# A reordered prologue: block 1's norm and half of the first B norm on VectorE, block 0's attention output stored in four parts

## The chip, the cores and the metric

The kernel runs on one core of a Trainium2 chip. The metric is the device time of one execution in microseconds (us). Executions of this kernel agree within about 0.2%. A comparison calls a version faster or slower only if it differs by more than 2%.

## The reference, cut to what matters

Two pairs of layers on 2048 tokens of width 1024: A is a dilated local attention with 32 heads and a window of 8 keys (every second token), B is a gated MLP of width 3584. Both stand behind a layer norm without parameters and add to the residual x.

```python
def _layernorm(x, axis=-1, eps=1e-5):
    m = jnp.mean(x, axis=axis, keepdims=True)
    v = jnp.var(x, axis=axis, keepdims=True)
    return (x - m) / jnp.sqrt(v + eps)
...
    x = A_x
    x = x + _A_ref(_layernorm(x, axis=-1), A_wqkv, A_wo)
    x = x + _B_ref(_layernorm(x, axis=-1), B_W_gate, B_W_up, B_W_down)
    x = x + _A_ref(...)      # the same again
    x = x + _B_ref(...)
```

## The kernel before

Tokens are worked on in four blocks of 512; a block has four tiles of 128 tokens (`TPB = 4`). The kernel is one list of timed events, `ev`: each step is a function with the time at which its author expects it, and the instructions are emitted in order of these times. TensorE's matmul groups and all transfers issued by SyncE are chained (`issue_after`), so each of these two queues runs strictly in the order of the list. A transfer that waits for its data holds back every transfer listed behind it.

The norm of a block, as it runs on ScalarE, with GpSimd computing (variance + eps) to the power −0.5; `turn` is the transposing transfer that makes the matmul operand `xnT` from the normalised `xn`:

```python
    def ln_steps(n, which, early=False):
        ...
        def stats(t):
            def f():
                ...
                nc.scalar.activation(xn, xt[:], ACT.Square, accum_out=sq)
                nc.scalar.activation(xn, xt[:], ACT.Identity, accum_out=sx)
                ...
                nc.gpsimd.tensor_tensor(rstd, vpe, neg_half[:, 0:1], op=ALU.pow)
                nc.scalar.activation(mr, sx, ACT.Copy, scale=-1.0 / D)
                nc.scalar.activation(nb, mr, ACT.Identity, scale=rstd)
            return f

        def apply(t):
            def f():
                nc.scalar.activation(hold["xn"][:, t, :], x_tiles[b * TPB + t][:], ACT.Identity,
                                     scale=hold["st"][:, t, 4:5], bias=hold["st"][:, t, 6:7])
            return f

        def turn(t=None):
            def f():
                if t is not None:
                    sp_dma(hold["xnT"][:, t, :, :], hold["xn"][:, t, :], True)
                else:
                    ...
```

The attention output of a block goes to DRAM and comes back transposed (`oT`), to be the operand of the output projection:

```python
    def store_o(n):
        def f():
            b = n % NB
            dst = bass.AP(tensor=o_d.tensor, offset=o_d[b * TPB:b * TPB + 1].offset, ap=[[DH * P, P], [1, DH * P]])
            sp_dma(dst, att[n]["o_hm"][:].rearrange("p d t -> p (d t)"))
        return f
```

The prologue of the schedule. `want_...` asks for 1 MB slabs of weights; its times say when the ring slot of a slab comes free, and with that where the load of a later slab stands in SyncE's queue. `ln1` is the norm ahead of an attention block, `ln2` the one ahead of the MLP ("B norm"), `sums1` are the products of q and k of block 1, on VectorE:

```python
    spread(v_steps(0, ln_a[0], "v0", early=True), t_v0, GRP)
    ln1(1, 22.0, 47.5, True, 5.0)
    ...
    ev.append((t_qk1 + 1.6 * GRP, lambda: softmax(0)))
    spread(pv_steps(0), t_qk1 + 10.0, 4.2)
    ln1(2, 60.0, t_qk1 + 15.0, True)
    ...
    want_v("v123", t_v3 + GRP * KC / 2, t_gu0)
    spread(v_steps(1, ln_a[1], "v123", True), t_v1, GRP)
    ln1(3, 85.0, t_v2 + 2.0, True)
    ...
    spread(v_steps(2, ln_a[2], "v123", True), t_v2, GRP)
    ev.append((t_v2 + 10.0, store_o(0)))
    ev.append((t_v2 + 10.1, load_o(0)))
    ...
    spread(sums1, t_qk1 + 46.0, 4.4)
    want_wo(0, t_v3, t_v3)
    spread(wo_steps(0), t_wo0, 2 * GRP)
    ln2(0, [t_wo0 + 2 * GRP * (t + 1) + 0.1 for t in range(TPB)])
    spread(v_steps(3, ln_a[3], "v123"), t_v3, GRP)
    ...                       # then the gate and up groups of the MLP of block 0
```

So TensorE's order in the stretch that matters is: V of blocks 1 and 2, output projection of block 0, V of block 3, first gate group, first up group, and from there on the long MLP.

## Time and profile before

The time before is 1652.67 us (median of 3 runs, 1652.44 to 1653.47). The profiled execution spans 1650.2 us. Two lines of its page: TensorE's busy time, and the shares of the chain of waits that ended last.

```profile
PE 1623.2 (98%) x7576; PEld 778.2 (47%) x7576; DVE 1048.1 (64%) x888; ACT 534.6 (32%) x1117; POOL 276.3 (17%) x220
...
PE 90%; issue 0%; DVE 0%; ACT 0%; DMA 0%
```

TensorE is busy 98% of the span, and 90% of the chain is TensorE. So there is little to gain but TensorE's waits and its slow stretches. These are TensorE's waits other than the start-up ones and two short ones, 0.7 and 0.5 us, ahead of logit reductions (the tile that the matmul makes, what it waited for, us in total, times, longest):

```profile
PE acc_wo L115 <- DMA oT<-o_d: 6.5, 1, 6.5
PE acc_g L115 <- issue: 2.4, 1, 2.4
PE acc_v L115 <- ACT vT L303: 1.7, 1, 1.7
```

And this is TensorE's timeline around them. The columns are start, duration, engine, line, what is made from what, how many matmuls of which form, and in brackets the wait before it:

```profile
92.88 13.98 PE L115 MATMUL acc_v<-xnT_a,w_v 128*128 128x512 bf16 x64
108.50 13.97 PE L115 MATMUL acc_v<-xnT_a,w_v 128*128 128x512 bf16 x64 [1.65 <-ACT vT L303]
129.03 16.73 PE L115 MATMUL acc_wo<-w_o,oT 128*128 128x512 bf16 x64 [6.55 <-DMA oT<-o_d]
145.59 13.98 PE L115 MATMUL acc_v<-xnT_a,w_v 128*128 128x512 bf16 x64
161.96 3.53 PE L115 MATMUL acc_g<-xnT_b,w_g 128*128 128x512 bf16 x8 [2.40 <-issue]
165.33 1.89 PE L115 MATMUL acc_u<-xnT_b,w_u 128*128 128x512 bf16 x8
```

Read the 64 matmuls of the output projection (`acc_wo`) against the 64 of V (`acc_v`): 16.73 us against 13.98, though they have the same form. They follow a wait of 6.55 us. The first 8 gate matmuls (`acc_g`) follow a wait of 2.40 us and take 3.53 us, the next group 1.89. A wait can cost twice: itself, and a slow clock after it. In windows of 1 us the granted clock was one half from the first matmul to about 165.3 us at the gate group (3.4 us), but to about 134.6 us at the projection (5.6 us). **From the first up group (165.33 us) to the end of the span are 1484.9 us**; this number will serve as a check on every version.

The first gate group waits for the last transposed tile of the B norm. In ScalarE's timeline the last `xn_b` is ready at 158.71 us; its transpose, issued at 158.74, took 3.1 us to land, and the group starts at 161.96. SyncE's queue shows that tile's transpose right behind it, alone, while the third gate slab had been issued 13 us before it:

```profile
145.78 0.37 SPq L104 DMA_DIRECT2D w_g<-in_B_W_gate_dram  x1
...
158.74 1.23 SPq L104 DMA_TRANSPOSE xnT_b<-xn_b  x1
```

### The profile page before, as it was taken

The numbers are of one execution on the slowest core, as the hardware profiler recorded it, in microseconds if no ns is written. First come the engines' busy times: TensorE is split into PE (matmuls) and PEld (weight loads), VectorE is DVE, ScalarE is ACT, GpSimd is POOL, SyncE is SP. The second block draws the span as 40 slices with busy tenths as digits, with TensorE's granted clock in tenths as the row PEclk, the third lists the DMA queues.
The fourth block names the chain that finished last, engine by engine and source line by source line (L and its number), as shares of the span: only waits on it lengthen the run. The fifth ranks groups of instructions, "written<-read, shape, count | busy, mean of one in ns | idle before, by whom it ended". The sixth has DMA issues, their size and how long they took to land.

```text
span 1650.2 us, 18654 instructions
## 1 busy us (share of the span) xinstructions
PE 1623.2 (98%) x7576; PEld 778.2 (47%) x7576; DVE 1048.1 (64%) x888; ACT 534.6 (32%) x1117; POOL 276.3 (17%) x220
## 2 busy tenths in 40 slices
PE   7998999999999999999999999999999999999999
PEld 4543445444454445444454444544445444444444
DVE  1798788978199844949459493694927948211211
ACT  6675412415132522325124151340513401131110
POOL 1341104401052101211042010420105100000000
PEclk9998999999999999999999999999999999999999
DMA  7477666764747474784846847477485774655451
GB/s 257 104 192 193 163 172 190 206 190 148 231 149 190 152 204 142 229 210 136 211 155 202 200 153 223 160 187 199 153 229 178 186 219 152 198 160 184 153 163 67
DMA packets 370791, 296.82 MB, mean 180 GB/s; under 512 B 142352, under 2 KB 351248, under 8 KB 369680
## 3 DMA queue, kind: packets, MB, share of 16 engines
q1 hardware_dynamic: 370416, 295.10, 62.3%
q8 instruction: 59, 0.97, 0.2%
q10 hardware_dynamic: 288, 0.52, 0.1%
q14 instruction: 28, 0.23, 0.0%
HBM read 256.77 MB, written 21.00 MB: 168 GB/s over the span
## 4 chain that ended last, share of the span: by engine, by line
PE 90%; issue 0%; DVE 0%; ACT 0%; DMA 0%
PE acc_g L115 24%; PE dacc L115 23%; PE acc_u L115 23%; PE acc_wo L115 6%; PE acc_k L115 5%; PE acc_q L115 5%; PE acc_v L115 3%; PE L L115 0%; DVE x L556 0%; ACT vT L303 0%; DMA xnT_b<-xn_b 0%
## 5 line engine op out<-in xcount | busy, mean ns | idle before, releaser
L115 PE MATMUL acc_g<-xnT_b,w_g 128*128 128x512 bf16 x1792 | 425.0, 380 | 2.4 <-issue 2.4
L115 PE MATMUL acc_u<-xnT_b,w_u 128*128 128x512 bf16 x1792 | 423.3, 379 | 0.0
L115 PE MATMUL dacc<-w_d,hT 128*128 128x512 bf16 x1792 | 388.1, 379 | 0.0
L528 ACT ACTIVATE r<-acc_g 128x512 bf16<-128x512 f32 x224 | 132.6, 594 | 699.4 <-PE acc_g L115 685.1
L529 DVE TENSOR_TENSOR hT<-acc_u,r 128x512 bf16<-128x512 f32 x224 | 153.5, 687 | 322.0 <-PE acc_u L115 308.3
L115 PEld LDWEIGHTS <-w_g 128*128 128x128 bf16 x1792 | 175.0, 98 | 216.4 <-issue 7.5
L115 PEld LDWEIGHTS <-w_u 128*128 128x128 bf16 x1792 | 175.4, 98 | 211.8 <-issue 0.6
L115 PEld LDWEIGHTS <-hT 128*128 128x128 bf16 x1792 | 175.3, 98 | 211.4
L399 DVE TENSOR_TENSOR t<-q,k 128x2048 f32<-128x2048 bf16 x98 | 223.6, 2289 | 9.8 <-ACT k L342 6.6
L409 DVE TENSOR_TENSOR ac<-ac,t 128x2048 f32<-128x2048 f32 x84 | 191.8, 2283 | 0.4
L347 POOL COPY kh<-k 128x14 bf16<-128x14 bf16 x64 | 85.5, 1341 | 452.4 <-ACT k L342 452.4
L556 DVE TENSOR_TENSOR x<-dacc,x 128x512 bf16<-128x512 f32 x64 | 42.5, 687 | 164.8 <-PE dacc L115 164.8
L461 DVE TENSOR_TENSOR pv<-a,vhm 128x4096 bf16<-128x4096 bf16 x64 | 145.2, 2282 | 0.0
L115 PE MATMUL acc_wo<-w_o,oT 128*128 128x512 bf16 x512 | 114.6, 385 | 6.5 <-DMA oT<-o_d 6.5
L223 POOL TENSOR_TENSOR st_b<-st_b,neg_half 128x1 f32<-128x1 f32 x32 | 66.4, 2080 | 323.0 <-ACT st_b L222 323.0
L223 POOL TENSOR_TENSOR st_a<-st_a,neg_half 128x1 f32<-128x1 f32 x36 | 51.4, 1427 | 359.1 <-ACT st_a L222 359.1
L115 PEld LDWEIGHTS <-oT 128*128 128x128 bf16 x512 | 50.6, 99 | 69.3 <-DMA oT<-o_d 7.3
L346 POOL COPY k<-kh 128x14 bf16<-128x14 bf16 x48 | 71.8, 1497 | 45.6 <-DVE t L399 45.6
L462 DVE TENSOR_TENSOR pv<-pv 128x2048 bf16<-128x2048 bf16 x64 | 77.4, 1215 | 0.2
L218 ACT ACTIVATE xn_b<-x 128x1024 bf16<-128x1024 bf16 x32 | 33.4, 1045 | 96.5 <-DVE x L504 96.5
L338 ACT CAST q<-acc_q 128x512 bf16<-128x512 f32 x64 | 37.4, 584 | 71.2 <-PE acc_q L115 71.2
L399 DVE TENSOR_TENSOR ac<-q,k 128x2048 f32<-128x2048 bf16 x14 | 32.0, 2287 | 39.9 <-ACT k L342 32.8
(121 smaller groups left out, 1190.8 us busy)
## 6 DMA issues: line engine op xcount, KB each, us to landing
w_g<-in_B_W_gate_dram SPq DMA_DIRECT2D x56, 1024.0 KB, 6.8
w_u<-in_B_W_up_dram SPq DMA_DIRECT2D x56, 1024.0 KB, 5.4
w_d<-in_B_W_down_dram SPq DMA_DIRECT2D x48, 1024.0 KB, 5.6
w_o<-in_A_wo_dram SPq DMA_DIRECT2D x16, 1024.0 KB, 7.3
vhm<-v_d SPq DMA_DIRECT2D x32, 284.0 KB, 6.8
v_d<-vT SPq DMA_DIRECT2D x8, 1024.0 KB, 8.5
o_d<-ohm SPq DMA_DIRECT2D x8, 1024.0 KB, 10.0
oT<-o_d SPq DMA_DIRECT2D x32, 256.0 KB, 4.2
```

Source lines behind the costliest of these rows:

```text
L115: tail_pe[0] = nc.tensor.matmul(*args, **kwargs).ins
L223: nc.gpsimd.tensor_tensor(rstd, vpe, neg_half[:, 0:1], op=ALU.pow)
L338: nc.scalar.copy(q[:], acc[:])
L346: nc.gpsimd.tensor_copy(k[:, 0:HALO], khalo[n - 1][:, c, :])
L347: nc.gpsimd.tensor_copy(khalo[n][:, c, :], k[:, BLK:BLK + HALO])
L399: nc.vector.tensor_tensor(t[:], i0, i1, op=ALU.mult)
L409: nc.vector.tensor_tensor(o, ac[:], t[:], op=ALU.add)
L461: nc.vector.tensor_tensor(tt[:], a_bc, v_sh, op=ALU.mult)
L462: nc.vector.tensor_tensor(tt[:, 0:4], tt[:, 0:4], tt[:, 4:8], op=ALU.add)
L528: nc.scalar.activation(r[:], acc[:], ACT.Relu)
L529: nc.vector.tensor_tensor(hold["hT"][:, j, :], accs["u"][:], r[:], op=ALU.mult)
L556: nc.vector.tensor_tensor(xs, ac[t], xs, op=ALU.add)
```

## The change

The intent: block 1's norm moves from ScalarE to VectorE, which idled from 13.5 to 39.4 us; the norms of blocks 2 and 3 move forward into the time so gained on ScalarE; tiles 2 and 3 of the first B norm go to VectorE and most of block 1's products move behind them; the attention output is stored in four parts, so that only the last quarter follows the last P·V step; transposes of the B norm are listed 2.5 us earlier. The core of the diff:

```diff
@@ ln_steps: stats(t) and apply(t)
+                if t in dve:
+                    hold[t] = ln_dve_stats(xt)
+                    return
...
+                if t in dve:
+                    mv, rstd = hold[t]
+                    nc.vector.tensor_scalar(hold["xn"][:, t, :], x_tiles[b * TPB + t][:], mv[:, 0:1], rstd[:],
+                                            op0=ALU.subtract, op1=ALU.mult)
+                    return
...
+    def ln_dve_stats(xt):
+        bst = stat_pool.tile([P, 2, 6], F32, tag="bst", name="bst")
+        nc.vector.bn_stats(bst[:, 0, :], xt[:, 0:512])
+        nc.vector.bn_stats(bst[:, 1, :], xt[:, 512:1024])
+        ...
+        nc.gpsimd.tensor_tensor(rstd[:], vpe[:], neg_half[:, 0:1], op=ALU.pow)
+        return mv, rstd
...
-    def store_o(n):
+    def store_o(n, g0=0, g1=NG):
...
-                ev.append((a + 9.0, turn(t)))
+                ev.append((a + 6.5, turn(t)))
...
-    ln1(1, 22.0, 47.5, True, 5.0)
+    ln1(1, 18.0, t_qk0 + 2.0, True, 2.6, range(TPB))
...
-    spread(pv_steps(0), t_qk1 + 10.0, 4.2)
-    ln1(2, 60.0, t_qk1 + 15.0, True)
+    ln1(2, 36.0, t_qk1 + 2.0, True, 5.0)
+    spread(pv_steps(0), t_qk1 + 12.0, 4.2)
+    for i in range(4):
+        ev.append((t_qk1 + 12.0 + 9.0 * (i + 1) + 1.0, store_o(0, 2 * i, 2 * i + 2)))
+    ev.append((t_qk1 + 12.0 + 9.0 * 4 + 1.1, load_o(0)))
+    ln1(3, 66.0, t_v2 + 9.5, True, 5.0)
...
-    ln1(3, 85.0, t_v2 + 2.0, True)
-    ev.append((t_v2 + 10.0, store_o(0)))
-    ev.append((t_v2 + 10.1, load_o(0)))
...
-    spread(sums1, t_qk1 + 46.0, 4.4)
+    spread(sums1[:5], t_qk1 + 50.0, 4.4)
+    spread(sums1[5:], t_v3 + 6.0, 4.4)
...
-    ln2(0, [t_wo0 + 2 * GRP * (t + 1) + 0.1 for t in range(TPB)])
+    ln2(0, [t_wo0 + 2 * GRP * (t + 1) + 0.1 for t in range(TPB)], None, (2, 3))
```

(The loads of x of blocks 2 and 3, the stores of V and the requests for slabs were moved in the list as well.)

More of the change, by code (lines that the diff above doesn't have):

```diff
@@ L202, in slab_events, with ln_steps @@
             events.append((slab_plan[i - RING][2] + 0.3 if i >= RING else 0.1 * i, f))
-    def ln_steps(n, which, early=False):
+    def ln_steps(n, which, early=False, dve=()):
         b = n % NB
@@ L243, in ln_steps @@
         return [stats(t) for t in range(TPB)], [apply(t) for t in range(TPB)], turn, hold
+    def ln_dve_stats(xt):
+        bst = stat_pool.tile([P, 2, 6], F32, tag="bst", name="bst")
+        nc.vector.bn_stats(bst[:, 0, :], xt[:, 0:512])
+        nc.vector.bn_stats(bst[:, 1, :], xt[:, 512:1024])
+        mv = stat_pool.tile([P, 2], F32, tag="mv", name="mv", bufs=4)
+        nc.vector.bn_aggr(mv[:], bst[:].rearrange("p a b -> p (a b)"))
+        vpe = stat_pool.tile([P, 1], F32, tag="vpe1", name="vpe1")
+        nc.vector.tensor_scalar(vpe[:], mv[:, 1:2], EPS, None, op0=ALU.add)
+        rstd = stat_pool.tile([P, 1], F32, tag="rstd1", name="rstd1", bufs=4)
+        nc.gpsimd.tensor_tensor(rstd[:], vpe[:], neg_half[:, 0:1], op=ALU.pow)
+        return mv, rstd
     def ln_first():
@@ L251, in ln_first @@
             if t % 2 == 0:
-                bst = stat_pool.tile([P, 2, 6], F32, tag="bst", name="bst")
-                nc.vector.bn_stats(bst[:, 0, :], xt[:, 0:512])
-                nc.vector.bn_stats(bst[:, 1, :], xt[:, 512:1024])
-                mv = stat_pool.tile([P, 2], F32, tag="mv", name="mv")
-                nc.vector.bn_aggr(mv[:], bst[:].rearrange("p a b -> p (a b)"))
-                vpe = stat_pool.tile([P, 1], F32, tag="vpe1", name="vpe1")
-                nc.vector.tensor_scalar(vpe[:], mv[:, 1:2], EPS, None, op0=ALU.add)
-                rstd = stat_pool.tile([P, 1], F32, tag="rstd1", name="rstd1")
-                nc.gpsimd.tensor_tensor(rstd[:], vpe[:], neg_half[:, 0:1], op=ALU.pow)
+                mv, rstd = ln_dve_stats(xt)
                 nc.vector.tensor_scalar(xn, xt[:], mv[:, 0:1], rstd[:], op0=ALU.subtract, op1=ALU.mult)
@@ L271, in ln_first @@
                 nc.vector.tensor_scalar(vpe[:], nvar[:], -1.0 / D, EPS, op0=ALU.mult, op1=ALU.add)
-                rstd = stat_pool.tile([P, 1], F32, tag="rstd1", name="rstd1")
+                rstd = stat_pool.tile([P, 1], F32, tag="rstd1", name="rstd1", bufs=4)
                 nc.gpsimd.tensor_tensor(rstd[:], vpe[:], neg_half[:, 0:1], op=ALU.pow)
@@ L467, in pv_steps @@
         return [f_(g) for g in range(NG)]
-    def store_o(n):
+    def store_o(n, g0=0, g1=NG):
         def f():
             b = n % NB
-            dst = bass.AP(tensor=o_d.tensor, offset=o_d[b * TPB:b * TPB + 1].offset, ap=[[DH * P, P], [1, DH * P]])
-            sp_dma(dst, att[n]["o_hm"][:].rearrange("p d t -> p (d t)"))
+            off = g0 * DG * P
+            size = (g1 - g0) * DG * P
+            dst = bass.AP(tensor=o_d.tensor, offset=o_d[b * TPB:b * TPB + 1].offset + off, ap=[[DH * P, P], [1, size]])
+            sp_dma(dst, att[n]["o_hm"][:].rearrange("p d t -> p (d t)")[:, off:off + size])
         return f
@@ L587, in zero_v, with ln1 @@
         sp_dma(bass.AP(tensor=v_d.tensor, offset=v_d.offset, ap=[[NTOK, P], [P * NTOK, KC], [1, HALO]]), zpad[:])
-    def ln1(n, at, turn_at, early=False, gap=3.0):
-        stats, apply, turn, hold = ln_steps(n, "a", early)
+    def ln1(n, at, turn_at, early=False, gap=3.0, dve=()):
+        stats, apply, turn, hold = ln_steps(n, "a", early, dve)
         ln_a[n] = hold
@@ L594, in ln1, with ln2 @@
         ev.append((turn_at, turn()))
-    def ln2(n, ats, turn_at=None):
-        stats, apply, turn, hold = ln_steps(n, "b")
+    def ln2(n, ats, turn_at=None, dve=()):
+        stats, apply, turn, hold = ln_steps(n, "b", False, dve)
         ln_b[n] = hold
@@ L608 @@
     GAP0 = 2.05
-    t_v0 = 15.0
+    t_v0 = 17.0
     t_qk0 = t_v0 + GRP * KC
@@ L616 @@
     t_gu0 = t_v3 + GRP * KC
-    ev.append((0.45, zero_v))
-    ev.append((0.5, lambda: load_x(1)))
     want_v("v0", t_v0 + GRP * KC / 2, t_qk0)
     want_qk("qk01", t_v1)
+    want_v("v123", t_v3 + GRP * KC / 2, t_gu0)
+    ev.append((0.45, lambda: load_x(1)))
+    ev.append((0.5, zero_v))
     spread(v_steps(0, ln_a[0], "v0", early=True), t_v0, GRP)
-    ln1(1, 22.0, 47.5, True, 5.0)
+    ln1(1, 18.0, t_qk0 + 2.0, True, 2.6, range(TPB))
+    ev.append((t_qk0 - 4.0, lambda: load_x(2)))
     ev.append((t_qk0 + 1.5, store_v(0)))
+    ev.append((t_qk0 + 2.1, lambda: load_x(3)))
     spread(qk_steps(0, ln_a[0], "qk01"), t_qk0, GAP0)
@@ L631 @@
     spread(load_v_steps(0), t_qk0 + 5.0, 6.0)
-    ev.append((50.0, lambda: load_x(2)))
-    spread(qk_steps(1, ln_a[1], "qk01"), t_qk1, GRP)
     ev.append((t_qk1 + 0.5 * GRP, reds[KC - 2]))
@@ L636 @@
     ev.append((t_qk1 + 1.6 * GRP, lambda: softmax(0)))
-    spread(pv_steps(0), t_qk1 + 10.0, 4.2)
-    ln1(2, 60.0, t_qk1 + 15.0, True)
-    ev.append((70.0, lambda: load_x(3)))
-    want_v("v123", t_v3 + GRP * KC / 2, t_gu0)
+    ln1(2, 36.0, t_qk1 + 2.0, True, 5.0)
+    spread(qk_steps(1, ln_a[1], "qk01"), t_qk1, GRP)
+    spread(pv_steps(0), t_qk1 + 12.0, 4.2)
[3 more added lines that the diff above has]
+    ln1(3, 66.0, t_v2 + 9.5, True, 5.0)
     spread(v_steps(1, ln_a[1], "v123", True), t_v1, GRP)
-    ln1(3, 85.0, t_v2 + 2.0, True)
-    ev.append((t_v2 + 3.0, store_v(1)))
+    ev.append((t_v2 + 9.6, store_v(1)))
     spread(v_steps(2, ln_a[2], "v123", True), t_v2, GRP)
-    ev.append((t_v2 + 10.0, store_o(0)))
-    ev.append((t_v2 + 10.1, load_o(0)))
     ev.append((t_wo0 + 3.0, store_v(2)))
     sums1, red1 = prod_sum_steps(1)
-    spread(sums1, t_qk1 + 46.0, 4.4)
+    spread(sums1[:5], t_qk1 + 50.0, 4.4)
+    spread(sums1[5:], t_v3 + 6.0, 4.4)
     want_wo(0, t_v3, t_v3)
     spread(wo_steps(0), t_wo0, 2 * GRP)
-    ln2(0, [t_wo0 + 2 * GRP * (t + 1) + 0.1 for t in range(TPB)])
+    ln2(0, [t_wo0 + 2 * GRP * (t + 1) + 0.1 for t in range(TPB)], None, (2, 3))
     spread(v_steps(3, ln_a[3], "v123"), t_v3, GRP)
```

## The prediction

> **What bounds the kernel now.** Engine shares: TensorE busy 1623 of 1650 us (98%). The chain of waits is 90% TensorE. Nothing can gain 2% (33 us) without fewer matmuls, and the change removes none: TensorE's order of groups stays identical. Only idle and slow time in the first 165 us is at stake. The waits and the TensorE timeline show it: some 12 us at start-up (untouched), 1.2 us at two logit reductions (40 to 47 us), 1.65 us at the V projection of block 2 (V copies queued on ScalarE behind block 3's norm), 6.55 us ahead of the output projection (oT, read back from DRAM), 2.4 us ahead of the first gate matmul (transpose of xn_b). After the last two, matmuls start 0.43 us apart instead of 0.216: the output projection's 64 took 16.7 us against 14.0, the first gate group 3.5 against 1.9. The Trainium skill, "TensorE: Matmul & The Clock Gate", Part 1, says an idle TensorE falls to half clock and needs about 3.4 us to recover; this trace agrees. At stake: about 16 us (1%).
>
> **What the change does.**
> 1. Block 1's norm goes to VectorE (per tile two statistics at 0.6 us, a 0.54 us apply), idle from 13.5 to 39 us: free. The norms of blocks 2 and 3 (about 4.2 us a tile on ScalarE) move forward to 30 to 77 us; with the copies (0.47 us each) they fill ScalarE there. The 1.65 us wait goes.
> 2. ScalarE's last norm steps wait for GpSimd's power operation, which sits out VectorE's two-input operations ([...]the skill, "SBUF — State Buffer", "Who interferes with whom", says so). Block 0's exponential stands behind these norms. Adding trace durations along each engine's new order I get it about 4 us later, and a 2.2 us product now stands inside the softmax. So P·V of block 0 ends near 117 us, against 111.2. Logit waits stay about 1.9 us.
> 3. The store in four 256 KB parts: only the last follows P·V, and block 3's transpose issue (4.8 us) moves behind the reload. Before: P·V end 111.2, store issued 118.4 (7.4 us to land), projection at 129.0. After (estimate): 117 + 3.3 + 4.3 = about 125, against TensorE ready at 120. The wait shrinks to perhaps 4 us, still with the slow clock; if step 2 is too pessimistic it nearly vanishes.
> 4. First B norm: tiles 2, 3 on VectorE, with products postponed. The transpose lands about when V of block 3 ends: 2.4 us and the slow gate group (1.7 us) mostly go. But the first up slab now queues behind the last two transposes: a 1 to 2 us wait at the first up group.
>
> The first up group starts at about 158.5 instead of 165.5; later nothing changes.
>
> **Prediction.** About 7 us saved: 1645.5 us, range 1640 to 1650. Faster by over 2%: 0.01; within 2%: 0.98; slower: 0.01.
>
> **What would show it.** Waits: none of TensorE for a V copy; a shorter one ahead of the output projection, oT as releaser; none at the first gate group, one for w_u instead. Timeline: exponential near 75 us (71.6 before), P·V ending near 117, the last o_d store issued within a microsecond. From the first gate group to the end: the same length within 2 us.
>
> **What would make it wrong.** If ScalarE runs through the norms without GpSimd waits, P·V ends near 113 and the time falls to about 1640. If x of blocks 2 and 3 lands late, ScalarE holds K copies back and the gain goes. If the small stores land slowly (over 7 us), step 3 gives nothing.

## The result, and the profile after

The changed kernel takes 1648.72 us (median of 4 runs, 1648.00 to 1649.55) against 1653.04 (4 runs) of the kernel before in the same rounds: ratio 0.9974, 95% interval 0.9957 to 0.9992 (about 1 to 7 us saved), which is "same". A ratio is the mean time of one kernel's fast runs over the mean time of the other's fast runs of the same rounds, so it is not quite the ratio of the medians. About 4.3 us were saved where 7 were predicted; the measured median lies inside the predicted range.

The same lines of the page after. The span is 1646.7 us. TensorE's busy time cannot be compared to the microsecond: some matmul records are missing from this trace (7527 instead of 7576). VectorE and ScalarE now stand in the chain with 7%: it leads back from the wait ahead of the first up group through the norms.

```profile
PE 1618.9 (98%) x7527; PEld 777.7 (47%) x7576; DVE 1058.7 (64%) x918; ACT 511.9 (31%) x1057; POOL 267.0 (16%) x220
...
PE 90%; DVE 4%; ACT 3%; DMA 1%; issue 1%; POOL 1%; SPq 0%; ACTq 0%; DVEq 0%; POOLq 0%
```

TensorE's waits after:

```profile
PE acc_g L115 <- issue: 6.2, 1, 6.2
PE acc_wo L115 <- DMA oT<-o_d: 1.7, 1, 1.7
...
PE acc_u L115 <- DMA w_u<-in_B_W_up_dram: 0.5, 1, 0.5
```

The two waits at logit reductions (1.2 and 0.5 us) were left out. The wait for the V copies is gone and the one for `oT` fell from 6.5 to 1.7 us, but the wait of the first gate group *grew* from 2.4 to 6.2 us, and the first up group waits for its weights. The timeline says what that did:

```profile
93.90 27.79 PE L115 MATMUL acc_v<-xnT_a,w_v 128*128 128x512 bf16 x128
123.38 13.99 PE L115 MATMUL acc_wo<-w_o,oT 128*128 128x512 bf16 x62 [1.69 <-DMA oT<-o_d]
137.21 13.98 PE L115 MATMUL acc_v<-xnT_a,w_v 128*128 128x512 bf16 x64
157.38 3.57 PE L115 MATMUL acc_g<-xnT_b,w_g 128*128 128x512 bf16 x8 [6.20 <-issue]
161.48 2.50 PE L115 MATMUL acc_u<-xnT_b,w_u 128*128 128x512 bf16 x8 [0.52 <-DMA w_u<-in_B_W_up_dram]
```

V of blocks 1 and 2 now run without a gap, and the projection runs at full speed behind its 1.69 us wait (13.99 us). V of block 3 ends at 151.19 us (137.21 + 13.98) instead of 159.57: TensorE was **8.4 us ahead**. Then it waits 6.2 us, and the 8 gate matmuls take 3.57 us. In the stretch of that group the granted clock (the column behind the busy times of the five engines, followed by the DMA share and GB/s) was one half:

```profile
157.00:161.50 4.50, 3.60 (x9) 1.04 (x10) 4.50 (x3) 3.97 (x8) 1.08 (x1) 0.50 0.98 322
```

The first up group starts at 161.48 us instead of 165.33, which is 3.9 us earlier, and 1485.2 us of span follow (1484.9 before). So the whole change in time is there at the first up group, as predicted, and half of what TensorE had gained by the end of V of block 3 was given back at one wait.

What ends this wait? The releaser "issue" says only that the profile shows no releaser for that matmul; the groups' list, where the weight loads of the same group stand, names the transpose of `xn_b`. These are the longer pieces of the chain of waits that leads to the first up group (start, duration, what):

```profile
148.24 2.54 POOL rstd L262
...
150.81 0.56 DVE xn_b L235
151.36 1.18 SPq L104
...
152.66 2.66 SPq L104
...
155.42 6.01 DMA w_u<-in_B_W_up_dram
```

The power on GpSimd (2.54 us, beside a two-input sum of block 1 on VectorE), then the apply of tile 3 (normalised at 151.36 us), then in SyncE's queue the rest of the third transpose's issue and the issue of the fourth, then the first up slab. SyncE's queue of transfers in full (a group of two transposes is one line):

```profile
140.31 6.57 SPq L104 DMA_TRANSPOSE xnT_b<-xn_b  x2
146.98 0.53 SPq L104 DMA_DIRECT2D w_u<-in_B_W_up_dram  x1
147.60 0.58 SPq L104 DMA_DIRECT2D w_g<-in_B_W_gate_dram  x1
148.28 7.04 SPq L104 DMA_TRANSPOSE xnT_b<-xn_b  x2
155.42 0.52 SPq L104 DMA_DIRECT2D w_u<-in_B_W_up_dram  x1
```

The third and fourth transposes are the 7.04 us line. Their issue alone took 4.26 and 2.66 us, where the issue of each of these four took 1.23 us before. From issue to landing (shortest, median, longest of the four; the kernel before, then the changed one):

```profile
DMA to landing us min/median/max: 3.0/3.2/4.7
DMA to landing us min/median/max: 3.0/3.9/8.1
```

The 8.1 us are the third transpose's, which landed at 156.4. The fourth could not be issued before the third's issue had ended: 1.3 us after its tile was ready. It then took 4.6 us and landed at about 157.3, and the gate group started at 157.38. Just ahead of the two stand two 1 MB slabs, which are of the second up and the third gate slab and are used much later. The DMA engines were full at that time: from 152 to 157 us they moved 299 GB/s at a share of 1.18 (above 1 where the times of packets overlap), and at that rate 2 MB take about 7 us (an estimate). The Trainium skill, "DMA: Bandwidth & Descriptors", section "Issuing engines are not separate DMA queues", says that all transfers run on the same 16 engines and interleave, whichever engine started them. This trace agrees as far as it goes: the slab issued at 147.60 us took 7.9 us to land, and the transpose issued at 148.28 took 8.1. But SyncE issued all of these, so nothing here shows transfers of other issuers. And behind the transposes the first up slab, which was listed last, was issued only at 155.42 us and took 6.01 us.

Two steps of the prediction can be read off at once. The exponential of block 0 stands at 76.13 us (71.59 before), because ScalarE first runs the norm of block 3 and waits for GpSimd in it: one power took 2.53 us (from 66.31) instead of 0.55, beside a two-input product on VectorE (66.12 to 68.43). In the kernel before, a small copy on GpSimd took 2.3 us beside such a product and 0.19 us elsewhere. The Trainium skill, "SBUF — State Buffer", section "Who interferes with whom", says that a VectorE instruction with two SBUF inputs contends with a GpSimd instruction that reads SBUF, and calls the contention an exclusive lock; these times agree. P·V ends at 117.8 us (111.2 before). And the last quarter of the output was stored at once and `oT` began to load at 120.28.

### The profile page after: what moved, and what is told of

Read it like the earlier page. It is cut to its first block, busy times and chain, and to the rows that moved or that the text cites. A ratio compares the mean times of both kernels' runs of the same rounds, so it can differ in the third digit from the quotient of the medians.

```text
span 1646.7 us, 18588 instructions
## 1 busy us (share of the span) xinstructions
PE 1618.9 (98%) x7527; PEld 777.7 (47%) x7576; DVE 1058.7 (64%) x918; ACT 511.9 (31%) x1057; POOL 267.0 (16%) x220
## 4 chain that ended last, share of the span: by engine, by line
PE 90%; DVE 4%; ACT 3%; DMA 1%; issue 1%; POOL 1%; SPq 0%; ACTq 0%; DVEq 0%; POOLq 0%
PE acc_u L115 24%; PE acc_g L115 23%; PE dacc L115 23%; PE acc_wo L115 6%; PE acc_k L115 5%; PE acc_q L115 5%; PE acc_v L115 4%; DVE pv L473 1%; DMA x<-in_A_x_dram 1%; DVE t L411 1%; DVE pv L474 1%; ACT xn_a L221 0%; ACT xn_a L222 0%; DVE ac L421 0%; DMA w_u<-in_B_W_up_dram 0%
## 5 line engine op out<-in xcount | busy, mean ns | idle before, releaser
L226 POOL TENSOR_TENSOR st_b<-st_b,neg_half 128x1 f32<-128x1 f32 x30 | 62.7, 2095 | 325.2 <-ACT st_b L225 325.2
L115 PE MATMUL acc_wo<-w_o,oT 128*128 128x512 bf16 x496 | 111.0, 379 | 2.5 <-DMA oT<-o_d 1.7
L226 POOL TENSOR_TENSOR st_a<-st_a,neg_half 128x1 f32<-128x1 f32 x32 | 44.0, 1376 | 339.8 <-ACT st_a L225 339.8
L358 POOL COPY k<-kh 128x14 bf16<-128x14 bf16 x48 | 67.5, 1406 | 53.4 <-DVE t L411 53.4
L315 ACT CAST vT<-acc_v 128x512 bf16<-128x512 f32 x64 | 36.9, 586 | 66.5 <-PE acc_v L115 66.5
```

What stands on the lines that cost most here:

```text
L115: tail_pe[0] = nc.tensor.matmul(*args, **kwargs).ins
L358: nc.gpsimd.tensor_copy(k[:, 0:HALO], khalo[n - 1][:, c, :])
```

## The experiments

The theory after this reading: (T1) the two norms on VectorE are what gains the time, block 1's through the exponential and the projection, the B norm's through the gate group; (T2) what TensorE gained was partly absorbed at the gate group, because tile 3 is normalised late (block 1's products and sums and a slowed power stand ahead of it) and because its transpose and the first up slab stand behind 2 MB of slabs that are not needed yet. Rivals are named with each run. Each kernel was run in five rounds beside the kernel before, and all results were correct. The runs came in three batches on two chips (e1 to e4; e5 to e8; e9 and e10); in them the kernel before had medians of 1653.42, 1652.33 and 1653.39 us. The changed kernel itself was not run again, so a difference in us between it and an experiment, or between batches, is good to about 1 us; the ratios allow for this.

### e1_whole: the output stored in one part again

```diff
-    for i in range(4):
-        ev.append((t_qk1 + 12.0 + 9.0 * (i + 1) + 1.0, store_o(0, 2 * i, 2 * i + 2)))
+    ev.append((t_qk1 + 12.0 + 9.0 * 4 + 1.0, store_o(0)))
```

> The changed kernel with block 0's attention output stored whole again (one 1 MB store behind the last P.V step, the reload behind it); everything else as changed. My theory (the time won ahead of the output projection is absorbed at the first gate group, which waits for the norm of the last tile and for the slab queue, not for TensorE): the projection starts at about 128.5 us instead of 123.4 and runs slowly (16.7 us), but the wait of 6.2 us ahead of the first gate group vanishes, the first up group starts within 1.5 us of 161.5, and the time is within 1.5 us of 1648.7. Rival (each microsecond saved ahead of the projection comes through to the end): about 5 us of wait and 2.7 us of slow clock come back, 1656.

Measured: 1648.89 us (1648.16 to 1650.18), ratio 0.9974 (0.9962 to 0.9987), the same as the changed kernel's. TensorE's waits in it:

```profile
PE acc_wo L115 <- DMA oT<-o_d: 3.3, 1, 3.3
PE acc_g L115 <- DMA xnT_b<-xn_b: 3.1, 1, 3.1
PE acc_u L115 <- DMA w_u<-in_B_W_up_dram: 2.0, 1, 2.0
```

The projection waits 1.6 us longer for `oT`, and its 64 matmuls take 15.67 us, but the gate group's wait shrinks from 6.2 to 3.1 us. The first up group stands at 161.73 us against 161.48. So the four-part store is worth nothing in the changed kernel: what it gains is absorbed at the gate group, as T2 says, and the rival falls. The size was missed: the projection started at 125.33 and not at 128.5, because the whole 1 MB store, which took 7.4 us from its issue to the reload before the change (118.37 to 125.75), took only 3.9 us (118.16 to 122.03). The DMA engines were less busy: their share from 111 to 125 us was 0.85 before, 0.37 in the changed kernel and 0.33 here. That this is why the store was quicker is argued from these shares; no run tests it.

### e2_slabs: the two later slabs behind the last two transposes

```diff
-    want_v("v123", t_v3 + GRP * KC / 2, t_gu0)
+    want_v("v123", t_v3 + 2.5, t_gu0)
...
-    want_wo(0, t_v3, t_v3)
+    want_wo(0, t_gu0, t_gu0)
```

> The changed kernel with only the order in the DMA queue changed: the first up slab goes ahead of the last two transposes of xn_b, and the two slabs that are needed only later (second up, third gate) go behind them. Theory A (the transposes stand behind 2 MB of weights in the queue and share the DMA engines with them): the last transpose is issued as soon as tile 3 is normalised (about 151.4 us) and lands 3.2 us later, the gate group starts near 154.6 instead of 157.4, no wait for w_u: 3.5 to 4.5 us saved, about 1644.5. Theory B (what holds the gate group is the late norm of tile 3, behind products on VectorE; the queue adds nothing): at most 1 us saved, 1648.

Measured: 1644.15 us (1643.50 to 1646.21), ratio 0.9946 (0.9934 to 0.9959). SyncE's queue now holds only the first up slab ahead of the third and fourth transposes:

```profile
146.47 0.53 SPq L104 DMA_DIRECT2D w_u<-in_B_W_up_dram  x1
147.09 5.13 SPq L104 DMA_TRANSPOSE xnT_b<-xn_b  x2
152.35 0.50 SPq L104 DMA_DIRECT2D w_g<-in_B_W_gate_dram  x1
152.95 0.55 SPq L104 DMA_DIRECT2D w_u<-in_B_W_up_dram  x1
```

The third transpose's issue took 2.42 us and the fourth's 1.34 us. TensorE:

```profile
154.35 2.94 PE L115 MATMUL acc_g<-xnT_b,w_g 128*128 128x512 bf16 x8 [3.56 <-DMA xnT_b<-xn_b]
```

Theory A held, and B's 1648 falls. Tile 3 is normalised 0.5 us earlier (150.85 us), as is everything in this profile from the exponential on, and yet the gate group starts 3.0 us earlier and the up group (157.08 us) waits for nothing. What is left of the gate group's wait, 3.56 us, is the fourth transpose's landing: it was issued at once and took 3.4 us. The edit also moved the first up slab forward, ahead of both transposes; the two moves were not run apart. Of the 4.4 us at the first up group 3.0 are there when the gate group starts; the rest is mainly the wait for `w_u` (0.52 us), which is gone, and the shorter slow gate group (2.94 us instead of 3.57). The order of transfers alone was worth about 4.6 us (1648.72 to 1644.15), which is as much as the whole change.

### e3_products: block 1's products behind the last norm

The products and sums of block 1 that stand between the norm steps of tiles 2 and 3 are chained behind the last apply of the B norm:

```diff
-    spread(sums1[5:], t_v3 + 6.0, 4.4)
+    def behind(f, tail):
+        def g():
+            with tc.issue_after(tail[0]):
+                f()
+        return g
+    spread([behind(f, norm_end) for f in sums1[5:]], t_v3 + 6.0, 4.4)
```

> The changed kernel with only VectorE's order changed: block 1's logit products from the sixth on stand behind the norm of tile 3, so no 2.3 us product is between the residual adds and the norm; the DMA queue is as changed. Theory B (late norm): tile 3 is normalised about 141 us instead of 151.4, the transposes land before V of block 3 ends (151.2), the gate group does not wait, and only the first up slab, still queued behind the transposes, costs a wait of some 2 us: 5 us saved, about 1643.5. Theory A (queue): the two transposes still sit behind the two slabs, the last lands at 154 to 155, the gate group starts there: about 3 us saved, 1646.

Measured: 1646.18 us (1645.92 to 1646.47), ratio 0.9958 (0.9944 to 0.9971). Tile 3 is normalised at 143.87 us instead of 151.36, 7.5 us earlier; the powers ahead of it took 0.56 us. But the gate group starts only 2.0 us earlier (155.34 us): its two transposes were issued from 146.10 on behind the same two slabs (144.79 and 145.41 us), the last issue ended at 153.2, and the first up slab was issued behind them again. So a tile that is ready is not a tile that has landed. Theory A's 1646 held; theory B's 1643.5 did not.

```profile
144.79 0.53 SPq L106 DMA_DIRECT2D w_u<-in_B_W_up_dram  x1
145.41 0.59 SPq L106 DMA_DIRECT2D w_g<-in_B_W_gate_dram  x1
146.10 7.13 SPq L106 DMA_TRANSPOSE xnT_b<-xn_b  x2
...
155.34 3.15 PE L117 MATMUL acc_g<-xnT_b,w_g 128*128 128x512 bf16 x8 [4.06 <-issue]
```

The first three lines are of SyncE's queue, the last of TensorE's timeline.

### e4_norm3late: statistics of block 3's norm behind the exponential

Block 3's `ln1` is split; its statistics are chained behind the exponential of block 0 and its applies follow at 80 us of the list.

```diff
-    ln1(3, 66.0, t_v2 + 9.5, True, 5.0)
+    s3, a3, turn3, ln_a[3] = ln_steps(3, "a", True)
+    spread([behind_exp(f) for f in s3], 70.0, 5.0)
+    spread(a3, 80.0, 5.0)
+    ev.append((t_v2 + 9.5, turn3()))
```

> The changed kernel with block 3's norm on ScalarE moved behind block 0's softmax exponential. Theory (the exponential stands behind norm steps that wait for GpSimd): the exponential runs near 72.5 us instead of 76.1, P.V ends near 114 instead of 117.8, the wait for oT (1.7 us) goes, and the waits at the logit reductions (1.7 us) shrink. By itself that saves little at the end, because the first gate group still waits for the norm and the transposes: 0 to 3 us, about 1647. Rival (the softmax is what bounds the prologue): P.V's 3.6 us come through, 1645 or below.

Measured: 1645.87 us (1645.39 to 1647.91), ratio 0.9957 (0.9945 to 0.9970). The exponential stands at 73.14 us instead of 76.13, P·V ends 2.9 us earlier (114.9), the wait for `oT` is gone, tile 3 is normalised at 148.86 and the first up group starts at 158.82 us, 2.7 us earlier. The time lies within the theory's 0 to 3 us, but its reason, that this saves little by itself, was wrong: nearly all of P·V's 2.9 us came through, as the rival had it. The path is VectorE's own queue, where P·V, block 1's first products, the adds of x behind the projection and the B norm stand in this order: the first add starts at 128.44 us instead of 131.39, 2.9 us earlier, though the projection starts only 1.3 us earlier (122.05).

### e5_prodslab: e2 and e3 together

> The changed kernel with both edits that worked alone: the row sums of block 1 that the products of the gates feed stand behind the last normalisation of block 0, and the 2 MB of later slabs stand behind the last two transposes. Theory (the first gate group waits because tile 3 is normalised at 151.4 us and its two transposes then stand behind the slabs in the queue; both must go): tile 3 normalised at about 144, transposes landed by about 148, gate group starts right at the end of V of block 3 (about 151.3) without a wait over 0.5 us and at full clock, first up group at about 153, time about 1640 (1638.5 to 1642). Rival (the two edits buy the same time, so they do not add): no more than the better one alone, 1644.

Measured: 1641.13 us (1640.60 to 1641.61), ratio 0.9930 (0.9918 to 0.9943). The first up group stands at 154.81 us. The edits add: 4.6 and 2.5 us alone, 7.6 together (in ratios 0.0028 and 0.0016, together 0.0044), so the rival's 1644 falls. One expected detail was missed: the gate group still waits 1.93 us, because its transposes, no longer behind the slabs, still stand behind one slab and each other (issued 145.49 to 150.94), and start at 153.08 rather than at 151.3.

### e6_all: e2, e3 and e4 together

> The three edits together: row sums late, slabs late, and the statistics of block 3's norm behind the exponential of block 0. Theory: V of block 3 ends about 1.4 us earlier than in the changed kernel (149.9), the gate group does not wait, time about 1638.7 (1637 to 1641), the fastest of all. Rival (the earlier exponential is absorbed again by a wait at the gate group): the same as the two edits without it, within 0.5 us.

Measured: 1638.73 us (1638.15 to 1639.57; 4 runs), ratio 0.9917 (0.9903 to 0.9930). TensorE has one short wait left in this stretch:

```profile
122.95 13.98 PE L117 MATMUL acc_wo<-w_o,oT 128*128 128x512 bf16 x64
136.76 13.98 PE L117 MATMUL acc_v<-xnT_a,w_v 128*128 128x512 bf16 x64
151.44 1.89 PE L117 MATMUL acc_g<-xnT_b,w_g 128*128 128x512 bf16 x8 [0.70 <-ACT vT L317]
153.16 1.89 PE L117 MATMUL acc_u<-xnT_b,w_u 128*128 128x512 bf16 x8
```

The projection does not wait. V of block 3 ends at 150.7 us (149.9 was expected), and the gate group waits 0.70 us (none was expected), for the last V copies, and then runs at full clock (1.89 us). The rival (absorbed again) falls: the earlier exponential is worth 2.4 us here too. With e9, which is the same within the noise, this is the fastest version, 0.8% below the kernel before and 0.6% below the changed kernel.

### e7_normb_act: the B norm back on ScalarE

```diff
-    ln2(0, [t_wo0 + 2 * GRP * (t + 1) + 0.1 for t in range(TPB)], None, (2, 3))
+    ln2(0, [t_wo0 + 2 * GRP * (t + 1) + 0.1 for t in range(TPB)], None, ())
```

> The changed kernel with one part undone: the first B norm wholly on ScalarE, as before, with the transposes still issued tile by tile. Theory (when tile 3 is normalised counts): tile 3 ready at 153 to 155 instead of 151.4, first up group at about 163 instead of 161.5, time 1650 to 1651.5. Rival (the DMA queue of slabs sets when the transposes land, whoever normalises): first up group within 0.3 us of 161.5, time 1648.7.

Measured: 1654.10 us (1652.33 to 1654.78), ratio 1.0009 (0.9995 to 1.0022). Undoing this one part takes back more than the whole gain. Both sizes were missed. Tile 3 is ready at 158.4 us and not at 153 to 155, because in ScalarE's queue the norm steps of the last tiles, which wait 2.01, 0.81 and 0.75 us for GpSimd's powers, stand between copies of V, and each holds the other back: V of block 3 waits 0.99 and 1.80 us for copies, ends at 156.5 instead of 151.2, and the gate group starts at 161.68 us with half clock. About 2.2 us of that later end arose earlier: the projection waited 2.21 us in this profile instead of 1.69 and ran 15.67 us instead of 13.99, so not all of the loss need be the norm's. The direction of the theory held, and the rival (the queue alone decides) falls.

### e8_norm1_act: block 1's norm back on ScalarE

```diff
-    ln1(1, 18.0, t_qk0 + 2.0, True, 2.6, range(TPB))
+    ln1(1, 18.0, t_qk0 + 2.0, True, 2.6)
```

> The changed kernel with another part undone: block 1's norm back on ScalarE. Theory: some 16 us of ScalarE work come back ahead of the exponential, which moves from 76.1 to 78 to 80 us, P.V ends at about 121 instead of 117.8, the oT wait of the projection grows from 1.7 to about 5 us and part of that is absorbed at the gate group: time 1650 to 1652. Rival (ScalarE has slack there and the exponential is held by VectorE alone): time 1648.7, exponential within 0.5 us of 76.1.

Measured: 1654.48 us (1653.51 to 1655.56), ratio 1.0012 (1.0000 to 1.0025). The exponential moved to 81.54 us and P·V's end to 123.3, both beyond the expected range. The wait for `oT` did not grow (0.8 us): TensorE itself was held up earlier, by 4.5 us ahead of the logit reductions and 1.1 us at q, and came to the projection at 128.1 us. The gate group starts at 163.09. ScalarE had no slack there; the rival falls.

### e9_all_whole: e6 with the output stored in one part

The edit is that of e1, made to the kernel of e6.

> The version with all three edits (1638.7 us), its attention output stored in one part instead of four. Theory (the four-part store was worth nothing in the changed kernel only because the gate group waited later for something else): with no wait at the gate left to absorb it, the later oT shows: the projection waits about 1.5 us for oT, the gate group's 0.7 us wait for the V copy stays or goes, time 1639.5 to 1640.5, that is 0.8 to 1.8 us slower. Rival (the store in parts is worth nothing anywhere): 1638.7, within 0.4 us.

Measured: 1638.58 us (1638.53 to 1638.73; 4 runs), ratio 0.9910 (0.9896 to 0.9923). This expectation was missed and the rival holds: the store in parts is worth nothing here either. In this version `oT` is not what the projection waits for. The one store is issued 0.02 us after P·V's end, the reload is issued at 118.72 us, and TensorE starts the projection at 122.03 without a wait, straight from V of block 2. Counted from the exponential, the reload is issued 1.4 us later than in e6 (45.6 against 44.2 us), but nobody was waiting for it.

### e10_no_vector: both norms back on ScalarE

The edits of e7 and e8 together. What is left of the change is the order of the prologue, and the store in parts.

> The changed kernel with both norms back on ScalarE: what is left of the change is the order of the prologue and the store in four parts. Theory (each norm is a link of one series: block 1's norm sets the exponential and the projection's start, the B norm sets the gate group after it): the two losses of the runs that undid one each add, 1648.7 + 5.4 + 5.8, about 1659.5 (1657 to 1661), slower than the kernel before; the exponential at about 81.5 us, the first gate group at about 167. Rival (the two losses are one and the same wait at the gate group, met twice): about 1654.5.

Measured: 1660.27 us (1657.98 to 1660.45), ratio 1.0037 (1.0024 to 1.0051): classed "same", but the whole interval lies above the kernel before. TensorE:

```profile
155.93 5.25 PE L115 MATMUL acc_v<-xnT_a,w_v 128*128 128x512 bf16 x16 [3.90 <-ACT vT L315]
161.66 1.89 PE L115 MATMUL acc_v<-xnT_a,w_v 128*128 128x512 bf16 x8 [0.48 <-ACT vT L315]
170.04 3.29 PE L115 MATMUL acc_g<-xnT_b,w_g 128*128 128x512 bf16 x8 [6.49 <-issue]
```

The exponential stands at 82.26 us, V of block 3 waits 3.90 us for copies, and the gate group starts at 170.04 (expected about 167). In ratios, e7 lies 0.0035 above the changed kernel and e8 0.0038; both together are 0.0063 above it, against a sum of 0.0073. So the two losses nearly add, as for two links of one series, and do not meet in one wait: the rival's 1654.5 falls.

### All versions side by side

Times in us; the ratio is to the kernel before of the same rounds. "V3 end" is the end of V of block 3, "tile 3" the time at which the last tile of the B norm is ready.

| version | median | ratio | V3 end | tile 3 | first gate | first up | span after first up |
|---|---|---|---|---|---|---|---|
| before | 1653.04 | 1 | 159.6 | 158.7 | 161.96 | 165.33 | 1484.9 |
| changed | 1648.72 | 0.9974 | 151.2 | 151.4 | 157.38 | 161.48 | 1485.2 |
| e1_whole | 1648.89 | 0.9974 | 154.8 | 151.7 | 157.89 | 161.73 | 1484.9 |
| e2_slabs | 1644.15 | 0.9946 | 150.8 | 150.9 | 154.35 | 157.08 | 1485.3 |
| e3_products | 1646.18 | 0.9958 | 151.3 | 143.9 | 155.34 | 159.55 | 1484.6 |
| e4_norm3late | 1645.87 | 0.9957 | 149.9 | 148.9 | 154.87 | 158.82 | 1484.9 |
| e5_prodslab | 1641.13 | 0.9930 | 151.2 | 143.9 | 153.08 | 154.81 | 1484.7 |
| e6_all | 1638.73 | 0.9917 | 150.7 | 144.4 | 151.44 | 153.16 | 1484.6 |
| e7_normb_act | 1654.10 | 1.0009 | 156.5 | 158.4 | 161.68 | 166.06 | 1486.3 |
| e8_norm1_act | 1654.48 | 1.0012 | 156.7 | 157.3 | 163.09 | 167.01 | 1485.4 |
| e9_all_whole | 1638.58 | 0.9910 | 149.8 | 143.5 | 150.15 | 151.87 | 1485.1 |
| e10_no_vector | 1660.27 | 1.0037 | 163.6 | 166.8 | 170.04 | 173.99 | 1484.7 |

The last column stays within 2 us over all twelve versions: everything that separates them happened before the first up group. (A profile is one execution, so its times carry that execution's scatter; the whole profile of e9 runs about 0.9 us ahead of that of e6 already at the exponential.)

## Why the prediction was right or wrong

- **Class, range and bound: right.** The time was called 1645.5, 1640 to 1650, "same" with 0.98; it came to 1648.72, near the upper end. TensorE stayed the bound, and only its waits in the first 165 us moved.
- **Step 1, block 1's norm is free and the V-copy wait goes: right.** That wait is gone from the list of waits. The prediction gave the step only those 1.65 us. e8 shows how much hangs on it in the new order: put back on ScalarE, it costs 5.8 us (1648.72 to 1654.48).
- **Step 2, the exponential 4 us later, P·V ending near 117: right**, with 76.1 (about 75 was said) and 117.8. The mechanism, ScalarE's queue behind a GpSimd power, is shown in the trace, and e4 shows that moving that norm behind the exponential brings back 3.0 us there and 2.9 us of time.
- **Step 3, the store in parts: the mechanism was right for the wait, its worth was not.** The wait for `oT` shrank to 1.7 us, less than the "perhaps 4 us, still with the slow clock", and the projection ran at full clock. But e1 and e9 show that the parts as such are worth nothing at the end. In the kernel before, the transpose of block 3 (issued at 112.83 us) held the store back to 118.37, 7 us after P·V's end; in the new order the store follows P·V at once (P·V ends at 118.14 us in e1, the store is issued at 118.16). This the prediction had. And a whole store then took 3.9 us instead of 7.4, beside less busy DMA engines; that those are the reason is not shown.
- **Step 4 is the one that failed.** The prediction put it as "The transpose lands about when V of block 3 ends: 2.4 us and the slow gate group (1.7 us) mostly go." Instead the last transpose landed about 6 us after V of block 3 ended, the gate group waited 6.2 us, and it took 3.57 us where it was to run at full clock. The wait is a sum of three terms: tile 3 was normalised 0.2 us after V of block 3 ended (151.36 and 151.19), its transpose was issued 1.3 us later because the third one's issue, 4.26 us instead of 1.23, held the queue, and it took 4.6 us to land. Two things were mis-sized. First, tile 3 was late: even with the landing of 3.2 us that was the median before, a wait of about 3.4 us would have been left (an estimate; e2, with the slabs out of the way, measured 3.56). "With products postponed" did not hold, since products and sums of block 1 still stood between the norm steps; e3 moved them behind and had tile 3 at 143.87, for 2.5 us of time. Second, the transposes stood behind 2 MB of slabs; e2 changed their order and gained 4.6 us. Both are shown, and e5 shows that they add. The prediction saw the first up slab behind the transposes, but not the other two slabs ahead of them.
- **The sum.** The first up group was predicted at 158.5 and came at 161.48: 3.0 us too late, which with the unchanged rest gives the 3.2 us by which the time was missed. The prediction's own figures (projection at 125, 16.7 us long, then 14.0 for V of block 3) put the gate group near 155.7, an estimate. It started 1.7 us later and ran 1.7 us longer than at full clock, while the wait for `w_u` was 0.5 us where 1 to 2 were foreseen: together about 2.4 of the 3.0 us. TensorE came to that wait earlier than predicted, but this neither helped nor hurt: in e1 V of block 3 ended at 154.8, near the predicted time, and the first up group still came at 161.73. So the time fell inside the range because the range was wide; the better step 3 did not bring it there.
- **What the change is made of.** The new order alone, with both norms on ScalarE, is slower than the kernel before (e10, +6.9 us in its rounds); moving the two norms wins that back and 4.3 us more. Neither norm alone suffices (e7, e8).
- **Open.** e10 was not split into the order and the store in parts; since e1 and e9 found the latter worth nothing in two orders, I take it to be the order, but this is argued and not shown.

## What to carry to other kernels

After each gain, ask what the engine will do with it: TensorE was 8.4 us ahead at the end of one stage and gave half back at the next wait, and the part that looked best in the list of waits (`oT`, 6.5 to 1.7 us) was worth nothing by itself. A transfer has a place in a queue as well as a size: before you cost it with the duration it has by itself, list what stands ahead of it in the new order and whether that is needed sooner, because the wrong order of three 1 MB weight slabs and two transposes cost as much here as the whole change gained. And when several small edits remove different links of one series, try them together: alone they gave 4.6, 2.5 and 2.9 us, together 10.0.

## What the Trainium skill lacked or had wrong

- "TensorE: Matmul & The Clock Gate", Part 1, gives half clock after at least one idle window of about 3.4 us, and says that the window runs freely. The runs show that the length of a wait does not decide by itself: after 2.40 us (kernel before) 8 gate matmuls took 3.53 us, and after 3.07 us (e1_whole) they took 1.89. It lacks the plain consequence that a wait shorter than the window can already cost the slow clock: in the kernel before it added 1.6 us to a wait of 2.4.
- "DMA: Bandwidth & Descriptors" gives, in its section "DMA Transpose (X-bar)", no duration of a transpose's issue or landing. Elsewhere the skill has a bandwidth of transposes, cycle counts of their instructions and the time of a single small one, but nothing for one that stands behind other transfers. Here a 256 KB transpose with nothing ahead of it took 1.23 us to issue and 3.0 us to land; right behind 2 MB of slabs the issue took 4.26 us and the landing 8.1.
- "SBUF — State Buffer", "Who interferes with whom", was right about GpSimd and two-input VectorE operations. What no page that I read gives is the power operation by itself: on 128x1 values it took 0.55 us undisturbed and 2.53 us beside a two-input product.
